# Attention, routed experts and a dense MLP on one Trainium2 core: the last MLP's matrix operands moved to other start addresses in SBUF

## The chip, the cores and the metric

One core of a Trainium2 chip runs the whole program. The metric is the device time of one execution in microseconds (us), less is better. The profile is one execution of the same program, recorded instruction by instruction.

## The reference

The program computes three stages, one after the other; the change touches the third.

```python
x = attention(q, k, v)                      # linear attention, 8 batches x 576 tokens, 512 wide
x = moe(x)                                  # 4608 tokens, each through one of 8 experts, 512 -> 1024 -> 512
h = x @ w_in                                # last MLP: 4608 x 512 by 512 x 2048
g = np.maximum(0.01 * h, h)
out = (g @ w_out).astype(np.float32)        # 4608 x 2048 by 2048 x 512
```

## The kernel before

Both products of the last MLP are split into a high and a low part (`hi`, `lo`, the type fp32r) and computed as hi*hi + hi*lo + lo*hi, so each block product is three matmuls per 128 rows of the contraction. On top of that each product is a Strassen-like scheme: 7 block products in the place of 8, numbered 1 to 7 and always run in the order 1, 2, 6, 7, 5, 3, 4 (`ORDER`).

A matmul has two operands in SBUF. `lhsT`, 128x128, is loaded into the array first (the profile shows this as an instruction of its own, PEld); `rhs`, here 128x256, is streamed through it. Every matmul of both products has its own load.

**The first product** (line L954, in `Hidden.product`) loads the weights and streams the tokens. It runs in units (m, q): 9 groups m of 512 tokens, and for each of them 4 quarters q of the weights. A unit is 7 products of 12 matmuls, 84 matmuls in all, and there are 36 units. The streamed operands of the products 1, 2 and 6 lie in the tile `x3`, those of 7, 5, 3 and 4 in `xh7`, `xl7`, `xh5` and so on. The loaded weights lie in `wi0` for q = 0 and in `wi1` for q = 1, 2, 3. The split into hi and lo is ScalarE's (L506) and VectorE's (L507).

**The second product** (line L1126, in `run` of `last_product`) loads the hidden values and streams the weights. It runs over 18 blocks s of 256 tokens; a block is 7 products of 24 matmuls, 168 in all. The two first blocks are interleaved, the others run one after the other. The loaded operand goes through a ring of three pairs of buffers (`ring`), made of spent parts of `wi0` and `x3`. The streamed weights lie in `wi0` (product 1), in `wi1` (products 2, 6, 7, 5) and in `wo3` and `wo4` (products 3 and 4). All these views are made in `views`.

**The token numbers**: the result rows are scattered by number. Per block a DMA loads 256 numbers into `idf[s % 2]` (L1078 in `load`), VectorE turns them into integers (`idi`, L1142), and GpSimd's indirect DMA scatters two times 128 rows (L1148).

The order of the work around the change is the order of the code; nothing is scheduled by costs. Tiles get their start addresses from pools: `pre` is laid out from the upper end of SBUF downwards (so its first tile is `xr0`, then `x3`, then `wi0` at the top), `pa`, `pa2` and `pb` one after the other from below.

The experts of the second stage (L663, L674) use the same type and the same three-matmul scheme with 512 streamed columns, in tiles named `xk`, `xv`, `xq`; their last, small groups run with 256 columns.

Of the kernel before, what the change touches and what calls it, by code (L numbers as in the profile page):

```python
# [9 lines left out]
F32 = mybir.dt.float32  # L10
# [22 lines left out]
C_ID, C_ONE, C_TRI, C_WD, C_EOFF, C_TOK, C_RST, C_K512, C_IOTA, C_E = 0, 128, 256, 384, 456, 464, 500, 740, 752, 768  # L33
# [856 lines left out]
class Hidden:  # L890
# [7 lines left out]
    def early(self, p, pw):  # L898
        self.xr[0] = p.tile([128, 4, 2 * TB], F32, name="xr0")
        self.x3 = p.tile([128, 3, 2, 2, TB], F32R, name="x3")  # L900
        for n, i in enumerate((1, 2, 6)):
            self.xh[i], self.xl[i] = self.x3[:, n, 0], self.x3[:, n, 1]
        self.w0 = pw.tile([128, 7, 1024], F32R, name="wi0")
        self.weights(self.w0, 0)

    def late(self, p, p2, ps):
        self.ps = ps
        self.w1 = p.tile([128, 21, 1024], F32R, name="wi1")
        for q in range(1, 4):
            self.weights(self.w1[:, 7 * q - 7:7 * q], q)  # L910
        self.xt = p.tile([128, 4096], F32, name="xt")
        self.xr[1] = self.xt[:, 0:2048].rearrange("p (k t) -> p k t", k=4)
        self.t = {i: self.xt[:, 2048 + 512 * n:2560 + 512 * n].rearrange("p (k t) -> p k t", k=2) for n, i in enumerate((4, 5, 6, 7))}
        for i in (7, 5, 3, 4):
            self.operand(p2, i)
        self.ht = [[p2.tile([128, 2, 2, TB], F32, name=f"ht{f}{i}") for i in range(3 - f)] for f in range(2)]
        self.s = [{n: p2.tile([128, 2, TB], F32, name=f"s{n}{i}") for n in (1, 6, 7, 5)} for i in range(2)]
# [108 lines left out]
        store(u, 1)  # L1026


def last_product(tc, did, hd, wops, out):

    nc, V = tc.nc, tc.nc.vector
    w, hr, S, ring, sv, yo, idf, idi = {}, [None, None], {}, [], [], [], [], []
# [3 lines left out]
    def wview(i, t):  # L1036
        w[i] = t.rearrange("p (h k f) -> p h k f", h=2, k=8)

    def views(hidden, p):

        w0, w1, x3, xr0 = hidden.w0, hidden.w1, hidden.x3, hidden.xr[0]
        half = lambda t: t.rearrange("p (k t) -> p k t", t=128)
        hr[0] = hidden.xt.rearrange("p (c t) -> p c t", t=TB)
        hr[1] = flat(w1, 1).bitcast(F32).rearrange("p (c t) -> p c t", t=TB)
        wview(1, flat(w0, 0))
        for n, i in ((0, 2), (2, 6), (3, 7), (4, 5)):
            wview(i, flat(w1, n))
        S[0] = p.tile([128, 8, 128], F32, name="S5")
        for n in range(2):
            S[1 + n] = xr0[:, 2 * n:2 * n + 2].rearrange("p a (b t) -> p (a b) t", t=128)  # L1050
        x3 = [x3[:, n].rearrange("p h k t -> p (h k t)") for n in range(3)]
        ring.append((half(w0[:, 4]), half(w0[:, 5])))
        ring.append((half(x3[0]), half(x3[1])))
        ring.append((half(w0[:, 6]), half(x3[2])))
        idf.extend(p.tile([128, 2, 2], F32, name=f"idf{i}") for i in range(2))

    def tiles(p):
        for i in range(2):
# [57 lines left out]
    def run(ps):  # L1116
        for i in (7, 5, 3, 4):
            wload(i)
        for n, (s, i) in enumerate(seq):
# [23 lines left out]
            else:  # L1143
# [3 lines left out]
                for t in range(2):  # L1147
# [3 lines left out]
                    tc.add_to_no_dep_group("out", ins.ins)  # L1151

    return views, tiles, late, ended, tail, run


@with_exitstack
def build(ctx: ExitStack, tc, a, out):
# [6 lines left out]
    did = dram.tile([NT + SLOT, 2], F32, name="did")  # L1164
    wops = {"win": [dram.tile([128, 7, 2, 2, 256], F32, name=f"wid{q}") for q in range(4)],
            "wout": dram.tile([7, 128, 2, 8, 256], F32, name="wod")}
    hd = dram.tile([NA, 4, 2, 128, 1024], F32, name="hd")
# [7 lines left out]
    with tc.manual_schedule():  # L1175
        cf = con.tile([128, CW], F32, name="cf")
# [40 lines left out]
        with actx:  # L1217
            tail, sp = attention(actx, pools, tc, cst, a, region, xd, first)
# [4 lines left out]
        with ExitStack() as sctx, ExitStack() as bctx:  # L1223

            def pre():
                p = sctx.enter_context(tc.tile_pool(name="pre", bufs=1, side="right", reuse_waits="tile"))
                hidden.early(p, p)
                hidden.xload(0)

                def loads():  # L1230
                    for i in ORDER:
                        hidden.wload(0, i)
                        yield

                return loads(), lambda: (hidden.prep(0, 1), hidden.prep(0, 2))

            with ectx, ExitStack() as rctx:
                rest(rctx, pre)
            views, tiles, late, ended, tail, run = last_product(tc, did, hd, wops, out)
            p = bctx.enter_context(tc.tile_pool(name="pa", bufs=1, reuse_waits="tile"))  # L1240
            with ExitStack() as hctx:
                ps = hctx.enter_context(tc.tile_pool(name="ps_w", bufs=2, space=PSUM, reuse_waits="tile"))
                hidden.late(p, hctx.enter_context(tc.tile_pool(name="pa2", bufs=1, reuse_waits="tile")), ps)
                views(hidden, p)
                for i in ORDER:
                    hidden.wload(1, i)
                hidden.xload(1)
                hidden.sums(0)
                for i in (6, 7, 5, 3, 4):
                    hidden.prep(0, i)  # L1250
                hidden.run(ended, tail)
            p = bctx.enter_context(tc.tile_pool(name="pb", bufs=1, reuse_waits="tile"))
            late(p)
            tiles(p)
            run(bctx.enter_context(tc.tile_pool(name="ps_b", bufs=2, space=PSUM, reuse_waits="tile")))
# [23 lines left out]
```

## Time and profile before

| what | value |
|---|---|
| median of 3 runs | 1349.68 us (1348.0 to 1351.29) |
| the profiled execution's own time | 1349.73 us |
| its span (first to last instruction) | 1348.0 us |
| first matmul of the first product | 617.56 us after the span's start |
| matmuls in the program's trace | 9185, of which 3024 in each of the two products |
| mean granted TensorE clock | 0.987 |

A row of the timeline gives the start of a run of like instructions, its length, the engine, line and tiles, and the count. The end of a matmul in the profile is modelled, and neighbours overlap; so the time that a matmul costs is read from starts: the difference between the starts of two rows, divided by the matmuls that lie between them. Names drop the buffer number: `hp<-xh,wi` is a matmul into `hp` whose operands are an `xh` tile and a `wi` tile.

### The profile page before, as it was taken

To read this page: it belongs to the slowest core of one execution; us is meant where nothing else is said; L and a number is where in the kernel's file an instruction comes from. 1 tells how busy PE (TensorE), PEld (TensorE's weight loads), DVE (VectorE), ACT (ScalarE), POOL (GpSimd) and SP (SyncE) were. 2 spreads that over 40 slices of the span, in tenths; PEclk is the share of its full clock that TensorE was granted. 3 is DMA by queue.
4 is the path that set the end of the run, shared out by engine and by line. 5 is a ranking of instruction groups with operands and counts; after the bars stand their busy time and mean duration, and the time that the engine had idled before them with its cause. 6 is when DMAs were issued, how large, how long until landed. Compare 5 with 4: busy or idle time off the path is not lost.

```text
span 1348.0 us, 23450 instructions
## 1 busy us (share of the span) xinstructions
PE 1296.3 (96%) x9185; PEld 1213.5 (90%) x9185; DVE 1039.9 (77%) x1380; ACT 583.0 (43%) x914; POOL 347.2 (26%) x283
## 2 busy tenths in 40 slices
PE   6999698999999999998999999999999999999998
PEld 6888677888888877888999999999989999999998
DVE  5789766787778878557888888888778778787775
ACT  4566435554555555463333233333233333433332
POOL 2227841011101110111434334344311121122121
PEclk9999898999999999999999999999989999999999
DMA  9876337879879887878832333432985344453430
GB/s 369 349 288 202 126 111 248 261 254 299 259 256 311 281 279 243 284 240 308 312 120 118 141 141 126 156 127 95 381 337 187 114 139 143 125 156 118 132 112 32
DMA packets 146442, 279.04 MB, mean 207 GB/s; under 512 B 18192, under 2 KB 69904, under 8 KB 145424
## 3 DMA queue, kind: packets, MB, share of 16 engines
q1 hardware_dynamic: 121536, 207.93, 46.2%
q10 hardware_dynamic: 17232, 48.48, 9.1%
q0 software_dynamic: 7552, 21.02, 4.5%
q8 instruction: 75, 1.23, 0.4%
q14 instruction: 47, 0.39, 0.1%
HBM read 181.07 MB, written 96.32 MB: 206 GB/s over the span
## 4 chain that ended last, share of the span: by engine, by line
PE 24%; issue 22%; POOL 5%; DMA 2%; DVE 0%; POOLq 0%; ACT 0%; SPq 0%; ACTq 0%
PE hp L954 24%; POOL out L1148 4%; DMA wi<-wid 1%; DMA hd<-ht 1%; POOL s L999 0%; DVE ht L968 0%; POOLq L1148 0%; POOL s L1000 0%; POOLq L1275 0%; ACT s L998 0%; DVE ht L1004 0%; DVE ht L1008 0%; SPq L924 0%; POOL ht L980 0%; ACTq L965 0%
## 5 line engine op out<-in xcount | busy, mean ns | idle before, releaser
L954 PE MATMUL hp<-xh,wi 128*128 128x256 f32 x1152 | 209.9, 280 | 0.9 <-DMA wi<-wid 0.9
L663 PE MATMUL hp<-xq,xk 128*128 128x512 f32 (+1 forms) x640 | 189.6, 380 | 3.6 <-DVE xr L262 2.5
L954 PEld LDWEIGHTS hp<-xh,wi 128*128 128x128 f32 x1152 | 178.7, 188 | 1.1 <-ACT xh L506 1.1
L954 PE MATMUL hp<-x,wi 128*128 128x256 f32 x1296 | 162.9, 284 | 3.6 <-ACTq L864 3.6
L954 PEld LDWEIGHTS hp<-x,wi 128*128 128x128 f32 x1296 | 159.4, 191 | 3.8 <-ACTq L864 3.8
L954 PE MATMUL hp<-xl,wi 128*128 128x256 f32 x576 | 161.4, 280 | 0.0
L1126 PE MATMUL yp<-wi,x 128*128 128x256 f32 x944 | 157.5, 282 | 0.9 <-DVE x L507 0.9
L629 POOL DMA_INDIRECT xg<-xd,idi x44 | 54.2, 1233 | 360.6 <-ACT xq L665 200.5
L674 PE MATMUL yp<-xq,xk 128*128 128x512 f32 (+1 forms) x400 | 142.4, 385 | 0.8 <-DVE xq L666 0.8
L663 PEld LDWEIGHTS hp<-xq,xk 128*128 128x128 f32 x640 | 118.0, 188 | 26.7 <-DVE xr L262 2.9
L1126 PE MATMUL yp<-wi,wi 128*128 128x256 f32 x960 | 139.8, 280 | 0.0
L1148 POOL DMA_INDIRECT out<-yo,idx x36 | 60.4, 1677 | 300.0 <-DVE idx L1142 279.5
L507 DVE TENSOR_TENSOR xv<-st,xk 128x1024 fp32r<-128x1024 f32 x81 | 99.6, 1231 | 48.8 <-ACT xk L506 48.3
L1126 PEld LDWEIGHTS yp<-wi,x 128*128 128x128 f32 x944 | 131.8, 190 | 1.4 <-DVE x L507 1.4
L1126 PEld LDWEIGHTS yp<-wi,wi 128*128 128x128 f32 x960 | 128.4, 189 | 0.0
L674 PE MATMUL yp<-xq,xv 128*128 128x512 f32 (+1 forms) x320 | 121.8, 381 | 0.0
L663 PE MATMUL hp<-xq,xv 128*128 128x512 f32 (+1 forms) x320 | 121.1, 378 | 0.0
L968 DVE SCALAR_TENSOR_TENSOR ht<-ht 128x1024 f32<-128x1024 f32 x72 | 113.2, 1582 | 1.9
L954 PEld LDWEIGHTS hp<-xl,wi 128*128 128x128 f32 x576 | 108.3, 188 | 0.0
L999 POOL TENSOR_TENSOR s<-s,s 128x512 f32<-128x512 f32 x36 | 49.4, 1372 | 189.0 <-DVE s L996 99.1
L506 ACT CAST xk<-st 128x1024 fp32r<-128x1024 f32 x84 | 87.6, 1045 | 15.8 <-ACT y L680 8.8
L674 PEld LDWEIGHTS yp<-xq,xk 128*128 128x128 f32 x400 | 75.2, 189 | 14.9 <-DVE xq L666 1.2
(214 smaller groups left out, 2512.0 us busy)
## 6 DMA issues: line engine op xcount, KB each, us to landing
st<-in_w SPq DMA_DIRECT2D x88, 512.0 KB
hd<-ht ACTq DMA_DIRECT2D x72, 512.0 KB
xt<-hd SPq DMA_DIRECT2D x18, 1024.0 KB
wi<-hd SPq DMA_DIRECT2D x18, 1024.0 KB
wi<-wid SPq DMA_DIRECT2D x28, 512.0 KB
v<-in_v SPq DMA_DIRECT2D x16, 650.0 KB
wi<-wod SPq DMA_DIRECT2D x5, 2048.0 KB
k<-in_k SPq DMA_DIRECT2D x16, 576.0 KB
```

The costliest lines, as they stand in the source:

```text
L506: nc.scalar.copy(out=hi, in_=src)
L507: (eng or nc.vector).tensor_tensor(out=lo, in0=src, in1=hi.bitcast(F32), op=ALU.subtract)
L629: nc.gpsimd.indirect_dma_start(out=xg[:, t], out_offset=None, in_=xd[0:n], in_offset=bass.IndirectOffsetOnAxis(ap=idis[s % 2][:, t:t + 1], ...
L663: nc.tensor.matmul(hp[:, rows], lhsT=w[:, k, 128 * f:128 * f + 128], rhs=x[:, k, rows], start=(n == 0), stop=(n == 11))
L674: nc.tensor.matmul(yp[:, rows], lhsT=w[:, f, 128 * d:128 * d + 128], rhs=h[:, rows], start=(n == 0), stop=(n == 23))
L954: self.nc.tensor.matmul(bank[:, g], lhsT=w[:, h, k, 128 * g:128 * g + 128], rhs=x[:, k], start=(n == 0), stop=(n == 5))
L968: V.scalar_tensor_tensor(out=c, in0=c, scalar=0.01, in1=c, op0=ALU.mult, op1=ALU.max)
L999: G.tensor_tensor(out=s[6], in0=s[6], in1=s[5], op=ALU.add)
L1126: nc.tensor.matmul(bank, lhsT=x[:, k], rhs=w[i][:, h, k], start=(c == 0), stop=(c == 23))
L1148: ins = nc.gpsimd.indirect_dma_start(out=out, out_offset=bass.IndirectOffsetOnAxis(ap=idi[s % 2][:, t:t + 1], axis=0), in_=y[:, t], in_off ...
```

## The change

Three edits: the pool `pre` gets a further tile of 96 bytes in a partition that nothing uses; the two tiles of token numbers `idf0` and `idf1` are no longer made, their place is the 8 first columns of a region of the constants (a triangle of ones, read once at the program's start into another tile); and that region is passed on.

```diff
@@ class Hidden, early
         self.w0 = pw.tile([128, 7, 1024], F32R, name="wi0")
         self.weights(self.w0, 0)
+        pw.tile([128, 24], F32, name="pad")
@@ last_product
-def last_product(tc, did, hd, wops, out):
+def last_product(tc, did, hd, wops, out, room):
...
-        idf.extend(p.tile([128, 2, 2], F32, name=f"idf{i}") for i in range(2))
+        idf.extend(room[:, 4 * i:4 * i + 4].rearrange("p (a b) -> p a b", a=2) for i in range(2))
@@ build
-            views, tiles, late, ended, tail, run = last_product(tc, did, hd, wops, out)
+            views, tiles, late, ended, tail, run = last_product(tc, did, hd, wops, out, cf[:, C_TRI:C_TRI + 128])
```

No instruction is added, removed or moved: the two built programs hold the same instructions in the same order on every engine, with the same waits. What differs is where tiles start. The table gives the start in a partition in bytes, and the remainder by 128; every slice that a matmul takes starts a multiple of 512 bytes further, so that the remainder is that of each operand.

| tile | use in matmuls | start before | by 128 | start now | by 128 |
|---|---|---|---|---|---|
| `x3` | first product, streamed (1, 2, 6); second, loaded (ring) | 188384 | 96 | 188288 | 0 |
| `wi0` | first product, loaded (q = 0); second, loaded (ring) and streamed (1) | 200672 | 96 | 200576 | 0 |
| `wi1` | first product, loaded (q = 1, 2, 3); second, streamed (2, 6, 7, 5) | 20352 | 0 | 20352 | 0 |
| `xh7` to `xl4`, 8 tiles | first product, streamed (7, 5, 3, 4) | 126912 and on | 64 | 126848 and on | 0 |
| `wo3`, `wo4` | second product, streamed (3, 4) | 126912, 143296 | 64 | 126848, 143232 | 0 |
| `xk`, `xv`, `xq` of the experts | loaded and streamed | 49664 to 146944 | 0 | the same | 0 |

`xr0`, which no matmul reads, goes from 96 to 0, and the tiles of `pa2` and `pb` for VectorE, ScalarE, GpSimd and DMAs (`ht`, `s`, `v`, `yo`, `idx`, `S7`) shift down by 64 bytes.

## Rows read from the trace of the kernel before

**Rows 1.** The page: busy time by engine, and the granted clock in 40 slices.
```profile
PE 1296.3 (96%) x9185; PEld 1213.5 (90%) x9185; DVE 1039.9 (77%) x1380; ACT 583.0 (43%) x914; POOL 347.2 (26%) x283
...
PEclk9999898999999999999999999999989999999999
```
**Rows 2.** Busy time by stretch, inside the first product and inside the second.
```profile
core 0: us, PE busy (x) PEld busy (x) DVE busy (x) ACT busy (x) POOL busy (x), PEclk, DMA share, GB/s
780.00:980.00 200.00, 200.00 (x1686) 200.00 (x1685) 163.50 (x190) 64.91 (x111) 82.35 (x61) 1.00 0.46 176
1010.00:1200.00 190.00, 190.00 (x1613) 190.00 (x1612) 150.95 (x185) 71.91 (x76) 34.47 (x20) 1.00 0.45 140
```
**Rows 3.** What TensorE waited for, 617 to 976 us and 975 to 1348 us.
```profile
PE hp L954 <- ACTq L864: 3.6, 1, 3.6
PE hp L954 <- DMA wi<-wid: 0.9, 1, 0.9
...
PE yp L1126 <- ACT wi L506: 2.2, 1, 2.2
PE yp L1126 <- DVE x L507: 0.9, 2, 0.5
```
**Rows 4.** Timeline of TensorE: two units of the first product, q = 3 and q = 0.
```profile
770.03 4.48 PE L954 MATMUL hp<-x,wi 128*128 128x256 f32 x36
774.35 0.28 PE L954 MATMUL hp<-xh,wi 128*128 128x256 f32 x1
...
780.01 4.48 PE L954 MATMUL hp<-x,wi 128*128 128x256 f32 x36
784.32 0.28 PE L954 MATMUL hp<-xh,wi 128*128 128x256 f32 x1
...
790.01 4.48 PE L954 MATMUL hp<-x,wi 128*128 128x256 f32 x36
```
**Rows 5.** Timeline of TensorE: one block of the second product, and the next one's start.
```profile
1105.10 3.03 PE L1126 MATMUL yp<-wi 128*128 128x256 f32 x24
1107.97 2.98 PE L1126 MATMUL yp<-wi,x 128*128 128x256 f32 x24
...
1113.60 2.98 PE L1126 MATMUL yp<-wi,wi 128*128 128x256 f32 x24
1116.42 2.98 PE L1126 MATMUL yp<-wi,x 128*128 128x256 f32 x24
1119.24 0.40 PE L1126 MATMUL yp<-wo,wi 128*128 128x256 f32 x2
...
1122.08 3.00 PE L1126 MATMUL yp<-wo,wi 128*128 128x256 f32 x24
1124.92 1.35 PE L1126 MATMUL yp<-wi,x 128*128 128x256 f32 x10
```
**Rows 6.** Timeline of TensorE: 256-column matmuls of the experts' last group.
```profile
589.48 0.40 PE L663 MATMUL hp<-xq,xk 128*128 128x256 f32 x2
589.72 0.28 PE L663 MATMUL hp<-xq,xv 128*128 128x256 f32 x1
...
599.56 0.40 PE L663 MATMUL hp<-xq,xk 128*128 128x256 f32 x2
599.80 0.28 PE L663 MATMUL hp<-xq,xv 128*128 128x256 f32 x1
```
**Rows 7.** Timeline of VectorE in the second product: a split of each ring buffer, the numbers' copy.
```profile
1108.45 1.23 DVE L507 TENSOR_TENSOR x<-xt,wi 128x1024 fp32r<-128x1024 f32 x1 [1.19 <-ACT wi L506]
1109.67 1.23 DVE L507 TENSOR_TENSOR wi<-xt,wi 128x1024 fp32r<-128x1024 f32 x1
...
1123.06 0.16 DVE L1142 CAST idx<-idf 128x2 int32<-128x2 f32 x1
```
**Rows 8.** Who waited for line L1142, the copy of the token numbers.
```profile
L1142 DVE CAST idx<-idf x18: 158/159/161, 1011.0 to 1340.6; 128x2 int32<-128x2 f32 x18
...
  POOL out L1148: 279.5, 18
```

## The prediction

> **What bounds the kernel now.** The page comes first [rows 1]: TensorE is busy 96% of the span, and the granted clock is near full nearly everywhere. Next come two stretches inside the last MLP [rows 2]: TensorE's busy time fills each to the last digit (200.00 of 200.00 us, 190.00 of 190.00), the clock is 1.00 (the 2.4 GHz level), and VectorE, the next busiest, has 163.50 and 150.95 us. Third, what TensorE waited for [rows 3]: 4.5 us in all in the first product, 3.1 us in the second, all at their beginnings. So from 617.56 us to the end the time is the sum of what 6048 matmuls cost, and a nanosecond (ns) on each of them is 6 us. Last, the pace, from differences of starts. The reader is to see that it is not the same everywhere, though type, shape and clock are.
>
> - First product, unit q = 3 [rows 4]: 36 matmuls that stream `x3` take 774.35 − 770.03 = 4.32 us, 120.0 ns each; the 48 that stream `xh`, `xl` take 780.01 − 774.35 = 5.66 us, 117.9 each. Unit q = 0, loaded from `wi0`: 4.31 us, 119.7 each, and 790.01 − 784.32 = 5.69 us, 118.5 each. A unit is 9.98 us (770.03 to 780.01) or 10.00 (780.01 to 790.01).
> - Second product, one block [rows 5]: product 1 takes 1107.97 − 1105.10 = 2.87 us, 119.6 ns each; products 2 and 6 together 1113.60 − 1107.97 = 5.63, 117.3; 7 and 5 together 1119.24 − 1113.60 = 5.64, 117.5; 3 and 4 together 1124.92 − 1119.24 = 5.68, 118.3. The block is 19.82 us.
> - Experts with 256 columns [rows 6]: from 589.48 to 599.56 us lie 28 groups of three, 84 matmuls in 10.08 us: 120.0 each.
>
> Against the starts of the two operands (remainders by 128, from the table of the change; loaded first, then streamed): (0, 96) 120.0; (0, 64) 117.9; (96, 96) 119.6 and 119.7; (96, 64) 118.3 and 118.5; (96, 0) 117.3 to 117.5; and (0, 0), the experts, 120.0.
>
> **The change part by part.** After it all 6048 matmuls are (0, 0). This pair occurs before only in the experts [rows 6], with the same type, width, clock level and three-matmul order. Two readings of the list are possible. One looks at the streamed start alone: 96 is slow, 64 better, 0 best; the experts don't fit. The other looks at both: where loaded and streamed operand have the same remainder the pace is 120, (96, 96) in the products and (0, 0) in the experts, and it is lower only in pairs that differ; (0, 96) is then a pair that gains nothing. I take the second: it leaves no row out, and its price is a row of just the state that the change makes.
>
> *First product.* A unit at 120.0 is 84 × 0.120 = 10.08 us. Of 36 units, 9 (q = 0) go from 10.00 to 10.08 and 27 from 9.98 to 10.08: 9 × 0.08 + 27 × 0.10 = 3.4 us more. Its streamed `x3` matmuls, which the change frees from 96, gain nothing by this reading; those of `xh`, `xl` lose.
>
> *Second product.* A block at 120.0 is 168 × 0.120 = 20.16 us against 19.82: 0.34 us, and 18 blocks give 6.1 us. The low end is product 1's own pace there, which is (96, 96) but only 119.6 [rows 5]: 168 × 0.1196 = 20.09, 18 × 0.27 = 4.9 us. I take 120.0, since product 1 follows a product of another pair and the experts' run is uniform, as the products will be.
>
> TensorE has no idle time that could take this in [rows 2]; the waits of [rows 3] stand at the beginnings and are set by other engines, so I leave them.
>
> TensorE's loads and streams meeting in SBUF is what this amounts to. The Trainium skill speaks against it: "TensorE: Matmul & The Clock Gate", section "Step-by-step: what each phase is for", has two independent read ports, and loading the next weights takes no read bandwidth from the running matmul; its gap for 256 columns at the high clock is 256 / 2.4 + 2.5 = 109 ns and knows no address. By that rule the sum would be 0; the trace disagrees at least in that there are paces from 117.3 to 120.0 at one width and clock [rows 4 to 6].
>
> *The token numbers.* Their DMA is the same, into another place, with the same waits; the copy is 0.16 us, 18 times, on VectorE [rows 7, 8], which is idle for about 39 us of the second stretch [rows 2]. Only the scatter waits for it, which TensorE does not wait for [rows 3]: nothing. If the numbers came late, only GpSimd's scatters would, except the last.
>
> *The other shifted tiles.* VectorE's split takes 1.23 us whether it writes `x3` or `wi0` and whatever it reads [rows 7]; nothing is taken for it. Should VectorE's work get some per cent slower, its 36 and 39 idle us [rows 2] cover it, and if faster nobody waits for it but at the second product's start (0.9 us [rows 3], the bound either way). The weight load that TensorE waited 0.9 us for [rows 3] lands in a tile that moves; that is its bound either way too.
>
> **Sum:** 3.4 + 6.1 = 9.5 us, on the profiled execution's 1349.73 us: **1359.2 us**, slower by 0.7%. That execution lies on the median of the runs (1349.68), so nothing is corrected. Own range of this case: from 3.4 + 4.9 less the two bounds of 0.9, which is 1356.2, to 9.5 plus 0.9 and the upper run's distance of 1.6, which is 1361.7.
>
> **The rivals.**
>
> *Faster: the streamed start alone sets the pace.* For it: within the two products the order 96, 64, 0 gives 120.0, 118.3 and 117.4 without exception, and (0, 96) = 120.0 needs no excuse. Against it: the experts, streamed at 0, run at 120.0 [rows 6]. It must hold that something else of theirs costs: by 512 bytes they start at 0, the changed operands at 384, as `wi1` does now. Price at 117.4 ns: a unit 9.86 us (84 × 0.1174) instead of 9.98 or 10.00, so 27 × 0.12 + 9 × 0.14 = 4.5 us; a block 19.72 instead of 19.82, so 18 × 0.10 = 1.8 us; together 6.3 us less: 1343.4 us. The point that decides: today's mean pace is (27 × 9.98 + 9 × 10.00 + 18 × 19.82) / 6048 = 118.4 ns; if (0, 0) at these addresses runs below that, the sign turns.
>
> *No difference.* Either the pace doesn't hang on the addresses at all but on which product follows which, or (0, 0) settles near 118.4, say with the first matmuls of a product quick and the rest at 120. 0.2% of the time, 2.7 us, is about what a measurement of this kernel tells from no change; it is 0.45 ns a matmul, so this case is a pace of 117.9 to 118.8: about 1349.7 us. The page's rule above gives this time too. Against it: the paces repeat with the operands' tiles, not with places in the order: product 1 with `wi0` is slow in both stretches, product 2 slow in the first product where it streams `x3`, quick in the second where it streams `wi1` [rows 4, 5]. That the change doesn't do what it says is excluded by the table of starts.
>
> **How the numbers follow.** Same remainders slow, as forecast: 0.69. Streamed start alone: 0.23; it has the plain order in its favour, and the experts' row against it is of other tiles. Nothing to see: 0.08. These are the chances of slower, faster and same. To leave out no more than 2 in 10 the range has to reach the faster case: from 1343.0 to 1361.7 us.
>
> **What would show it.** In the changed profile: the unit 10.08 us and the block 20.16 us, all products alike at 120.0 ns. The faster rival shows 9.86 and 19.72, alike at 117.4. Both products unlike each other would mean that more than the remainder by 128 counts. VectorE's and the DMAs' waits for the numbers should read as before; a new wait of TensorE of more than a us would make the working wrong whatever the pace.

## The result, and the profile after

| | before | after |
|---|---|---|
| median, runs on the same chip | 1348.0 us (1346.89 to 1351.29, 5 runs) | 1358.94 us (1357.59 to 1361.05, 5 runs) |
| ratio | | 1.0067, 95% interval 1.0052 to 1.0081 |
| span of the profiled execution | 1347.96 us | 1357.12 us |
| start of the first product, of the second, of the last matmul | 617.56, 979.61, 1342.75 us | 616.30, 983.20, 1351.91 us |

The change makes the kernel slower by 0.7%: 9.0 us of 1348.0 by the ratio, 10.9 by the two medians. All line numbers after L900 are one higher than before.

The page, and the two stretches of [rows 2]:

```profile
PE 1304.4 (96%) x9185; PEld 1221.4 (90%) x9185; DVE 1041.1 (77%) x1380; ACT 583.4 (43%) x914; POOL 348.3 (26%) x283
...
PEclk9999898999999999998999999999999999999999
```

```profile
780.00:980.00 200.00, 200.00 (x1669) 200.00 (x1668) 162.97 (x189) 64.29 (x111) 81.56 (x60) 1.00 0.44 169
1010.00:1200.00 190.00, 189.36 (x1579) 189.16 (x1578) 149.20 (x182) 71.58 (x76) 34.82 (x20) 1.00 0.42 135
```

TensorE fills the first stretch as before, at the same granted clock of 1.00, but with 1669 matmuls where [rows 2] has 1686. The page's 96% tells nothing of this: an engine whose every instruction got longer looks as busy as ever.

TensorE's timeline, the same two units of the first product as in [rows 4], then a block of the second product as in [rows 5]:

```profile
771.52 4.48 PE L955 MATMUL hp<-x,wi 128*128 128x256 f32 x36
775.84 0.28 PE L955 MATMUL hp<-xh,wi 128*128 128x256 f32 x1
...
781.60 4.48 PE L955 MATMUL hp<-x,wi 128*128 128x256 f32 x36
785.92 0.28 PE L955 MATMUL hp<-xh,wi 128*128 128x256 f32 x1
...
791.68 4.48 PE L955 MATMUL hp<-x,wi 128*128 128x256 f32 x36
```

```profile
1110.11 3.04 PE L1127 MATMUL yp<-wi 128*128 128x256 f32 x24
1112.99 3.04 PE L1127 MATMUL yp<-wi,x 128*128 128x256 f32 x24
...
1130.27 1.00 PE L1127 MATMUL yp<-wi,x 128*128 128x256 f32 x7
```

A unit is 10.08 us (771.52 to 781.60 to 791.68), a block 20.16 us (1110.11 to 1130.27). Inside them all is alike: 36 matmuls in 4.32 us, 48 in 5.76, 24 in 2.88 (1110.11 to 1112.99), each 120.0 ns.

What TensorE waited for, first product and then second, and who waited for the copy of the token numbers:

```profile
PE hp L955 <- ACTq L864: 3.5, 1, 3.5
PE hp L955 <- DMA wi<-wid: 0.8, 1, 0.8
PE hp L955 <- DVE ht L969: 0.2, 1, 0.2
```

```profile
PE yp L1127 <- ACT wi L506: 2.5, 2, 2.0
PE yp L1127 <- DVE x L507: 1.4, 2, 0.8
PE yp L1127 <- DVE wi L507: 0.8, 1, 0.8
```

```profile
L1143 DVE CAST idx<-cf x18: 157/158/160, 1014.3 to 1349.7; 128x2 int32<-128x2 f32 x18
...
  POOL out L1149: 284.5, 18
```

The waits are those of [rows 3] with 1.6 us more at the start of the second product (4.7 instead of 3.1 in all, the new one behind VectorE's `wi` 0.8); the numbers' copy is 158 ns and waited for as in [rows 8].

The 9.16 us between the spans are made of three differences of the starts above. The first product takes 366.90 us instead of 362.05 (+4.85), the second 368.71 instead of 363.14 (+5.57), and the first product begins 1.26 us earlier.

### The profile page after: what moved, and what is told of

Read it like the earlier page. It is cut to its first block, busy times and chain, and to the rows that moved or that the text cites. A ratio compares the mean times of both kernels' runs of the same rounds, so it can differ in the third digit from the quotient of the medians.

```text
span 1357.1 us, 23450 instructions
## 1 busy us (share of the span) xinstructions
PE 1304.4 (96%) x9185; PEld 1221.4 (90%) x9185; DVE 1041.1 (77%) x1380; ACT 583.4 (43%) x914; POOL 348.3 (26%) x283
## 3 DMA queue, kind: packets, MB, share of 16 engines
q8 instruction: 75, 1.23, 0.4%
## 4 chain that ended last, share of the span: by engine, by line
PE 24%; issue 23%; POOL 5%; DMA 2%; DVE 0%; POOLq 0%; ACT 0%; SPq 0%; ACTq 0%
PE hp L955 24%; POOL out L1149 4%; DMA wi<-wid 1%; DMA hd<-ht 1%; POOL s L1000 0%; DVE ht L969 0%; POOLq L1149 0%; POOL s L1001 0%; POOLq L1276 0%; ACT s L999 0%; DVE ht L1005 0%; DVE ht L1009 0%; SPq L925 0%; POOL ht L981 0%; ACTq L966 0%
## 5 line engine op out<-in xcount | busy, mean ns | idle before, releaser
L955 PE MATMUL hp<-xh,wi 128*128 128x256 f32 x1152 | 213.5, 283 | 0.8 <-DMA wi<-wid 0.8
L955 PEld LDWEIGHTS hp<-xh,wi 128*128 128x128 f32 x1152 | 182.4, 192 | 1.0 <-ACT xh L506 1.0
L1127 PE MATMUL yp<-wi,wi 128*128 128x256 f32 x960 | 142.8, 283 | 1.2 <-DVE wi L507 0.8
L663 PEld LDWEIGHTS hp<-xq,xk 128*128 128x128 f32 x640 | 117.8, 188 | 26.8 <-DVE xr L262 3.1
L1000 POOL TENSOR_TENSOR s<-s,s 128x512 f32<-128x512 f32 x36 | 49.4, 1373 | 193.4 <-ACT s L999 117.5
```

What stands on the lines that cost most here:

```text
L663: nc.tensor.matmul(hp[:, rows], lhsT=w[:, k, 128 * f:128 * f + 128], rhs=x[:, k, rows], start=(n == 0), stop=(n == 11))
L955: self.nc.tensor.matmul(bank[:, g], lhsT=w[:, h, k, 128 * g:128 * g + 128], rhs=x[:, k], start=(n == 0), stop=(n == 5))
L1000: G.tensor_tensor(out=s[6], in0=s[6], in1=s[5], op=ALU.add)
L1127: nc.tensor.matmul(bank, lhsT=x[:, k], rhs=w[i][:, h, k], start=(c == 0), stop=(c == 23))
```

## The experiments

Each timed kernel ran beside the kernel before on the same chip, and ratios are taken against that. That neighbour's median was between 1342.4 and 1348.6 us from one comparison to the next, so a time here is compared only with its own neighbour.

### Pairs of starts, by themselves

A program of matmuls alone: for each pair of starts 12 matmuls to begin with, then 48 with the pair, every one with its own load.

```python
for k, (n, s, m) in enumerate(pairs()):          # columns, loaded start, streamed start
    for count, nm in ((WARM, "warm"), (RUN, name(n, s, m))):
        t = ps.tile([128, n], F32, tag="b%d%d" % (k % 2, count == RUN), name=nm)
        for j in range(count):
            nc.tensor.matmul(t, lhsT=w[:, s + 128 * (j % 16):s + 128 * (j % 16) + 128],
                             rhs=x[:, m + n * (j % 8):m + n * (j % 8) + n], ...)
```

> Measured by itself, the pace of fp32r matmuls by the start of both operands. This kernel computes nothing of the reference: it fills two tiles with numbers of one input, runs 12 + 48 matmuls for each pair of starts (a load of 128 columns before each), and writes one tile of sums to all rows of the output. The loaded operand starts at 0, 16, 32, 64 or 96 bytes past a multiple of 128, the streamed one at steps of 4 or 16 bytes; 256 columns, and eight pairs with 512. Theory 1 (the two starts against each other): streamed = loaded gives 120.0 ns at 0, 32, 64 and 96 alike, also where they differ by whole multiples of 128 bytes; loaded 0 with streamed 64 gives 117.8, loaded 96 with streamed 0 gives 117.4, loaded 96 with streamed 64 gives 118.3, and what counts is the difference of the two by 128, so that all pairs with a difference of 32 give 117.4 and all of 64 give 117.8. Theory 2 (the streamed start alone): the pace is the same for all loaded starts. For 512 columns: 226.7 ns at (0, 0) as in the experts; by theory 1 some ns less where the starts differ, by theory 2 as well only if the start is other than 0.

TensorE's timeline; the letters behind y are loaded and streamed start in words of 4 bytes (a = 0, i = 32 bytes, C = 112), and a pace is the distance to the next "warm" row by 48:

```profile
218.18 5.60 PE L50 MATMUL yaC<-x,w 128*128 128x256 f32 x48
223.62 1.63 PE L50 MATMUL warm<-x,w 128*128 128x256 f32 x12
...
260.97 5.92 PE L50 MATMUL yii<-x,w 128*128 128x256 f32 x48
266.73 1.59 PE L50 MATMUL warm<-x,w 128*128 128x256 f32 x12
```

(32, 32) is 5.76 / 48 = 120.0 ns, (0, 112) is 5.44 / 48 = 113.3, and so is (64, 0). For starts at multiples of 32 bytes the pace follows the difference, streamed less loaded, by 256:

| difference | 0 | 32 | 64 | 96 | 128 | 160 | 192 | 224 |
|---|---|---|---|---|---|---|---|---|
| ns, 256 columns | 120.0 | 116.7 | 117.8 | 120.0 | 118.6 | 117.4 | 113.3 | 118.3 |

Equal starts give 120.0 at 32, 64 and 96 as at 0, so the slow thing is not the multiple of 128. (The row of (0, 0) is the first group of the program and begins with seven steps of 205 to 214 ns, at the 1.2 GHz level of the clock; from the fourteenth step on it too runs at 120.0.) The period is 256 bytes, not the 128 by which the prediction sorted the pairs: (0, 128) is 118.6, (0, 256) 120.0. By 256 the starts before were `x3` and `wi0` 224, `wi1` 128, `xh` and `wo` 192, and the table gives every pace of the kernel before to 0.4 ns:

| operands (loaded, streamed) | difference | by the table | measured in [rows 4, 5] |
|---|---|---|---|
| `wi1`, `x3` | 96 | 120.0 | 120.0 |
| `wi1`, `xh` | 64 | 117.8 | 117.9 |
| `wi0`, `x3`; ring, `wi0` | 0 | 120.0 | 119.7, 119.6 |
| `wi0`, `xh`; ring, `wo` | 224 | 118.3 | 118.5, 118.3 |
| ring, `wi1` | 160 | 117.4 | 117.3 to 117.5 |

The changed kernel has 0 everywhere, since all its tiles start at 128 by 256.

### The token numbers alone

```diff
-        idf.extend(p.tile([128, 2, 2], F32, name=f"idf{i}") for i in range(2))
+        idf.extend(room[:, 4 * i:4 * i + 4].rearrange("p (a b) -> p a b", a=2) for i in range(2))
```

Without the further tile, `xh` and `wo` move to 0 (by 128), `x3` and `wi0` stay at 96.

> The second edit alone: the numbers' tiles are moved, the 96 bytes at the top are not added. Starts by 128: xh to xl and wo3, wo4 at 0, x3 and wi0 stay at 96, wi1 at 0. Theory 1 (starts against each other): in units with q = 1 to 3 the 48 matmuls of xh, xl become (0, 0), 120.0 ns, x3 stays at (0, 96), 120.0: unit 10.08 us against 9.98; in q = 0 they become (96, 0), 117.4: 9.94 against 10.00; in the second product products 3 and 4 become (96, 0), 117.4: block 19.78 against 19.82. Sum 27 x 0.10 - 9 x 0.06 - 18 x 0.04 = +1.4 us. Theory 2 (streamed start alone): xh, xl at 117.4 in all units, 9.95 for q = 1 to 3; sum about -2 us.

1351.51 us (9 runs) against 1348.64 (18): ratio 1.0020, 1.0008 to 1.0033. The unit is 10.07 us for q = 1 to 3, 9.96 for q = 0, the block 19.775. That is the differences again: `xh` behind `wi1` goes from 64 to 0 and loses 2 ns, behind `wi0` and with `wo` behind the ring from 224 to 160 and gains 1. This part of the change makes the first product slow and would make the second a little quicker.

### The upper tiles alone

```diff
+        pw.tile([128, 24], F32, name="pad")
...
+        p2.tile([128, 16], F32, name="padc")
...
+        p.tile([128, 16], F32, name="padd")
```

`x3` and `wi0` go to 0 and tiles of 64 bytes keep `xh` and `wo` at 64. One tile `s1` and the numbers lie in the constants to make room.

> The first edit alone: x3 and wi0 at 0, wi1 at 0, xh to xl and wo3, wo4 at 64 as in the kernel before (to make room, one of the first product's s1 tiles and the token numbers lie in the spent constants, and 64 bytes are left free below). Theory 1 (starts against each other): first product: x3 (0, 0), 120.0, xh and xl (0, 64), 117.8, in all units: 9.97 us; second: products 1, 2, 6, 7, 5 (0, 0) at 120.0, products 3 and 4 (0, 64) at 117.8: block 20.06 against 19.82, 18 x 0.24 = +4.3 us, units -0.3 us, together about +4 us. Theory 2 (streamed start alone): x3 at 117.4, unit 9.88; block 19.75: together about -4.5 us.

1354.36 us (10 runs): ratio 1.0037, 1.0022 to 1.0053. The unit is 9.98 us, the block 20.06. Product 7 and the start of product 5 in one block:

```profile
1115.94 3.04 PE L1129 MATMUL yp<-wi,wi 128*128 128x256 f32 x24
1118.82 3.04 PE L1129 MATMUL yp<-wi,x 128*128 128x256 f32 x24
```

These 24 take 2.88 us, 120.0 ns each, where [rows 5] has 117.5. Here the second product is slow: `wi1` behind the ring goes from 160 to 0. Its streamed start never moved; only the loaded one did, which by the rival of the streamed start alone changes nothing. Each part of the change is a loss by itself.

### All starts equal at 64

```diff
-        pw.tile([128, 24], F32, name="pad")
+        pw.tile([128, 8], F32, name="pad")
...
+        p.tile([128, 16], F32, name="pad1")
```

(Against the changed kernel.) All matmul tiles at 64 by 128.

> As the changed kernel, but all operands start at 64 past a multiple of 128 (32 bytes less at the top, 64 bytes free ahead of wi1). Theory 1 (starts against each other): equal starts again, 120.0 ns everywhere, unit 10.08, block 20.16, the time of the changed kernel, about 9.5 us over the kernel before. Theory 2 (streamed start alone): streamed at 64, 117.9 to 118.3 everywhere: unit 9.92, block 19.85, about 2 us below the kernel before.

1359.63 us (4 runs): ratio 1.0066, 1.0040 to 1.0092, units 10.08 us, blocks 20.16, every matmul 120.0: the changed kernel's numbers at another remainder.

### More differences, and 512 columns

The first program with streamed starts from 128 to 252 bytes, other loaded starts, and 512 columns.

> As the first kernel of pairs (it too computes nothing of the reference), with other pairs: 256 columns, loaded at 0, streamed at 128 to 252 bytes by steps of 4; five pairs with other loaded starts; and 512 columns, loaded at 0, streamed at 0 to 248 by steps of 8, and six pairs more. Theory 1, as the first kernel of pairs left it: the pace is a function of streamed minus loaded start by 256 bytes. So with 256 columns 128 gives 118.6, 160 gives 117.4, 192 gives 113.3, 224 gives 118.3, and so do (128, 64) and (192, 128) give 113.3 and (192, 0) at a difference of 64 gives 117.8. Theory 2, the streamed start alone, would give (128, 64) and (0, 64) the same 117.8. With 512 columns equal starts give 226.7 at 0, 64 and 128 alike; whether a difference gives less than 226.7 is open: the eight pairs measured so far don't (228.8 to 234.2).

```profile
131.69 5.60 PE L49 MATMUL yaabq<-x,w 128*128 128x256 f32 x48
137.13 1.64 PE L49 MATMUL warm<-x,w 128*128 128x256 f32 x12
...
282.72 11.04 PE L49 MATMUL zaaaa<-x,w 128*128 128x512 f32 x48
293.60 2.96 PE L49 MATMUL warm<-x,w 128*128 128x512 f32 x12
```

(0, 192) is 113.3 ns, and so are (128, 64), with 112 (64, 176) and (96, 208), and (0, 144). (192, 128), which is 192 too, is 117.8: a first sign of what came later, passed over here. Nothing at 256 columns is below that, and the slowest is 123.3, at streamed starts that are multiples of 4 bytes only. With 512 columns it is the other way round: equal starts, here (0, 0), are the quickest at 10.88 / 48 = 226.7 ns, at 64 and at 128 as well, and all differences cost 2 to 13 ns more, up to 240.0 at 88 bytes.

### All matmuls at the difference 192

```diff
-        self.x3 = p.tile([128, 3, 2, 2, TB], F32R, name="x3")
+        self.x3f = p.tile([128, 12 * TB + 80], F32R, name="x3")
...
-            x3 = [x3[:, n].rearrange("p h k t -> p (h k t)") for n in range(3)]
+            x3 = [hidden.x3f[:, 32 + 1024 * n:32 + 1024 * n + 1024] for n in range(3)]
+            r0 = {n: hidden.w0f[:, 16 + 1024 * n:16 + 1024 * n + 1024] for n in (4, 5, 6)}
...
+        p2.tile([128, 48], F32, name="padc")
```

Padding puts `xh` and `x3` 192 behind the weights; in the second product the ring lies in the same tiles at starts shifted by 128 and 64 bytes, so that the loaded operands again differ from the streamed ones by 192.

> The kernel with all 6048 matmuls of the last MLP at a difference of 192 bytes (streamed minus loaded, by 256): x3 and xh to xl at 64, wi0, wi1, wo3 and wo4 at 128, the ring's views at 192, by shifting tiles and by views that begin 64 or 128 bytes later. Theory 1: 113.3 ns everywhere, unit 9.52 us against 9.98, block 19.04 against 19.82: 36 x 0.46 + 18 x 0.78 = 30.6 us below the kernel before, about 1318 us, if VectorE (8.2 us of work in a unit, 15.8 in a block) and the loads keep up; a few us more if they don't. Theory 2 (streamed start alone, by 128): the streamed operands are at 64 in the first product, 0 in the second: 117.9 and 117.4, about 1345 us.

1333.26 us (1323.65 to 1341.29, 12 runs): ratio 0.9926, 0.9899 to 0.9954. In the profile of its quickest execution units are 9.52 us and blocks 19.04 (84 and 168 at 113.3), but the two first blocks take 57.00 us where they took 46.24. And the time of that execution, 1323.65 us, is one of six between 1323.7 and 1328.7; the six others lie between 1337.8 and 1341.3, which one pace for one difference does not explain. TensorE's waits at the start of the second product, and ScalarE's timeline there:

```profile
PE yp L1131 <- ACT wi L506: 12.5, 2, 10.1
```

```profile
977.56 0.37 ACT L1135 COPY v<-yp 128x256 f32<-128x256 f32 x1 [14.31 <-DMA hd<-ht]
977.83 1.05 ACT L506 CAST wi<-xt 128x1024 fp32r<-128x1024 f32 x1
```

ScalarE's copy into `v10` waited 14.31 us for the DMA out of a tile `ht`, and the splits that TensorE needed stood behind it. The padding had moved `v10` onto the last 192 bytes of the old `ht11`. This is the sort of wait that the prediction feared of moved tiles; the changed kernel's profile has none like it.

### 192 without the overlap

```diff
+        p.tile([128, 48], F32, name="pade")
```

> The kernel with a difference of 192 bytes, with 192 bytes left free ahead of the second product's v tiles, so that v no longer lies over the end of the tile whose store is the last of the first product. Theory (the wait of 10.1 us at the second product's start came from that overlap: ScalarE's copy into v waited for the store hd<-ht): the wait goes, the first two blocks take 45 to 47 us instead of 57.0, units stay 9.52 and blocks 19.04, and the time is about 10 us under the run with the overlap, 27 to 31 us (2.0 to 2.3%) under the kernel before. Rival (the wait is the price of the faster first product: the weights' loads or the stores come too late by their bandwidth): the first two blocks stay at 55 us or more.

1327.47 us (1317.91 to 1329.32, 5 runs) against 1343.51: ratio 0.9878, 0.9857 to 0.9898. The long wait goes, so the rival that the faster first product causes it falls. In the quickest execution units are 9.52 and blocks 19.04 as worked out, and the first two blocks take 49.06 us where 45 to 47 were expected. The median is 16.0 us under its neighbour, not the 27 to 31 expected. But the five times lie 11 us apart, and those of the kernel with the overlap 18, where the changed kernel and its parts have 3 to 7.

### The same program, two more executions

> The same kernel as the run before, for a second profile, since its five times lie between 1317.9 and 1329.3 us and the first profile is of the shortest. Theory: the pace is fixed by the starts (units 9.52, blocks 19.04 again), and what varies is the waits at the two places where TensorE waits for transfers, the first four units (42.7 us in the first profile) and the two first blocks (49.06 us). Rival: the pace itself differs between executions, and units or blocks in the middle are longer than 9.52 and 19.04.

> A third profile of the same kernel, with the same expectations: units 9.52 and blocks 19.04 in the middle, and differences only at the two beginnings.

1325.25 and 1334.58 us beside 1342.38. Rows of the timeline, of the first of the two and then of the second: two unit starts, and two neighbouring products of a block.

```profile
750.77 4.40 PE L958 MATMUL hp<-x,wi 128*128 128x256 f32 x36
760.66 4.40 PE L958 MATMUL hp<-x,wi 128*128 128x256 f32 x36
...
1114.39 2.88 PE L1132 MATMUL yp<-wi,wi 128*128 128x256 f32 x24
1117.11 2.88 PE L1132 MATMUL yp<-wi,x 128*128 128x256 f32 x24
```

```profile
741.49 4.24 PE L958 MATMUL hp<-x,wi 128*128 128x256 f32 x36
751.01 4.24 PE L958 MATMUL hp<-x,wi 128*128 128x256 f32 x36
...
1115.71 2.99 PE L1132 MATMUL yp<-wi,wi 128*128 128x256 f32 x24
1118.54 2.99 PE L1132 MATMUL yp<-wi,x 128*128 128x256 f32 x24
```

One has units of 9.89 us (117.8 ns) and blocks at 2.72 / 24 = 113.3; the other units of 9.52 and blocks at 117.8 (19.79 us each), to the last block. So my theory of one pace for one difference falls: at 192 there are two, and a product of the MLP keeps the one that it settles on near its beginning. A whole product at the slower pace costs some 13 us (36 × 0.37, or 18 × 0.75), which is the distance between the two groups of times of the kernel with the overlap (means of 1325.8 and 1338.7). That this is their cause is not shown, since none of its slower executions was profiled.

### One product of each unit and block at the difference 0

```diff
-        self.x3 = self.x3f[:, 0:12 * TB].rearrange("p (n h k t) -> p n h k t", n=3, h=2, k=2)
+        self.x3 = [self.x3f[:, o:o + 1024].rearrange("p (h k t) -> p h k t", h=2, k=2) for o in (16, 1088, 2112)]
...
-        wview(1, flat(w0, 0))
+        wview(1, hidden.w0f[:, 16:16 + 4096])
```

> As the run e7, but in every unit and every block product 1 has equal starts (difference 0, the pace that has been 120.0 in every profile), the other six a difference of 192. Theory 3 (at 192 there are two lasting paces, 113.3 and 117.8, and which one holds is decided when the stream of matmuls starts after a wait): each unit and block enters the 192 anew, out of the same pace of 120, so all units are alike, and so are all blocks, in every execution; if the entry falls on the quick pace, unit 12 x 0.120 + 72 x 0.1133 = 9.60 us, block 24 x 0.120 + 144 x 0.1133 = 19.20, and the time about 1316 us with a spread under 5 us in the runs; if it falls on the other, 9.92 and 19.84, about 1345. Rival (the pace is drawn by the execution, not by the entry): units of 9.60 in one stretch and 9.92 in another, and times as far apart as in e7 (11 us).

1322.81 us (1321.78 to 1325.33, 5 runs) against 1343.65: ratio 0.9852, 0.9838 to 0.9866. The spread is 3.5 us instead of 11. In the profile all units but the first and the fourth are 9.60 us, and all blocks but the two first 19.20:

```profile
749.74 4.32 PE L958 MATMUL hp<-x,wi 128*128 128x256 f32 x36
759.34 4.32 PE L958 MATMUL hp<-x,wi 128*128 128x256 f32 x36
...
1142.09 3.02 PE L1132 MATMUL yp<-wi 128*128 128x256 f32 x24
1144.95 2.90 PE L1132 MATMUL yp<-wi,x 128*128 128x256 f32 x24
...
1150.41 2.88 PE L1132 MATMUL yp<-wi,wi 128*128 128x256 f32 x24
1153.13 2.88 PE L1132 MATMUL yp<-wi,x 128*128 128x256 f32 x24
```

Product 1 runs at 2.86 / 24 = 119.2 ns, the others come back to 113.3 behind it each time (1150.41 to 1153.13). The slow product costs 0.08 us a unit and 0.16 a block, and the case of 117.8 (about 1345 us) came in none of the five runs. The 1316 us expected did not come either: units and blocks alone would give 36 × 0.38 + 18 × 0.62 = 24.8 us less than before, measured are 20.8, since the fourth unit (12.58 us, before 11.15) and the two first blocks (46.75, before 46.24) gained nothing.

### Each difference after waits

The first program without the 12 matmuls ahead; instead each group of 41 waits some us for VectorE, ten times with growing waits.

> Pairs again, without the reference's computation: ten differences (0 to 224 by 32, 112 and 144), each ten times with 41 matmuls, and ahead of each time TensorE has to wait for VectorE, by waits of ten lengths. Theory 3: a difference of 0 gives 120.0 ten times of ten; 192 gives 113.3 in some and 117.8 in others; which of the others have two paces is open. Rival: one pace per difference, as the first two kernels of pairs showed, where nothing waited.

TensorE's timeline at 192; the bracket is the wait ahead of the group:

```profile
523.62 4.93 PE L53 MATMUL yy<-x,w 128*128 128x256 f32 x41 [2.16 <-DVE x L50]
530.93 5.09 PE L53 MATMUL yy<-x,w 128*128 128x256 f32 x41 [2.38 <-DVE x L50]
```

4.93 us is a first step of 0.22, then steps that come down to 113.3 ns, and the last one's 0.28; in 5.09 the steps come to 117.8. So with the same operands a start after a wait can lead to either pace. The two groups differ in the wait, in the copies on VectorE that make it and in the output buffer, and three other groups with the second one's buffer have 113.3; what it is in the wait that decides stays open. Groups of 6.5 us and more ran for a part at the 1.2 GHz level (213 ns a matmul) and are left out. Of the groups at the full clock, by the last 24 steps, difference 0 has 120.0 in every one, 64 has 117.8, 96 has 120.0, 192 has 113.3 six times and 117.8 once, 32 has 116.7 or 117.8, 144 has 116.7 or 118.7, and 112 has 113.3 in all six.

### All matmuls at the difference 112

```diff
-        self.x3 = self.x3f[:, 0:12 * TB].rearrange("p (n h k t) -> p n h k t", n=3, h=2, k=2)
+        self.x3 = self.x3f[:, 4:12 * TB + 4].rearrange("p (n h k t) -> p n h k t", n=3, h=2, k=2)
...
-        p2.tile([128, 48], F32, name="padc")
+        p2.tile([128, 208], F32, name="padc")
+        self.xf = p2.tile([128, 4096 + 8], F32R, name="xh")
```

(Against the kernel at 192.) All of `x3` and `xh`, and the views of the second product's weights, start 16 bytes into their tiles.

> All 6048 matmuls at a difference of 112 bytes (streamed less loaded start, remainder by 256), by padding tiles and by views that start 16 bytes into their tile; the work is otherwise that of the changed kernel. The matmuls alone, after waits, gave 113.3 ns at 112 in every clean repetition, where 192 gave 113.3 or 117.8. Theory (the difference alone sets the pace, and 112 has one pace where 192 has two): units 84 x 0.1133 = 9.52 us, blocks 19.04 us in every stretch, 36 x (9.98 - 9.52) + 18 x (19.82 - 19.04) = 30.6 us less than before, some 3 back for the start of the second product: 1315 to 1320 us, and runs within 4 us of each other. Rival one (112 has two paces like 192): runs spread over 10 us and more, median 1325 to 1335. Rival two (16-byte starts cost something of their own in the kernel, with fp32r tiles that VectorE and ScalarE write): units above 9.6 us throughout, or VectorE's splits above 1.23 us and new waits of TensorE.

1329.17 us (1327.51 to 1330.85, 4 runs) against 1348.03: ratio 0.9855, 0.9829 to 0.9880. Rows of two usual units, a late one, and two neighbouring products of a block:

```profile
768.62 4.24 PE L960 MATMUL hp<-x,wi 128*128 128x256 f32 x36
...
778.14 4.24 PE L960 MATMUL hp<-x,wi 128*128 128x256 f32 x36
...
902.42 4.40 PE L960 MATMUL hp<-x,wi 128*128 128x256 f32 x36
...
912.10 4.24 PE L960 MATMUL hp<-x,wi 128*128 128x256 f32 x36
...
1144.47 2.88 PE L1137 MATMUL yp<-wi,wi 128*128 128x256 f32 x24
1147.19 2.88 PE L1137 MATMUL yp<-wo,x 128*128 128x256 f32 x24
```

The paces are as expected, units 9.52 us, every block from the third on 19.04 (113.3), and the runs within 3.3 us. So neither rival shows: there is no second pace, and VectorE's splits still take 1.23 us. The time was not: 18.9 us less than its neighbour where 27 were expected. I had counted the gain on all 36 units and 18 blocks. Two of the first units take 12.58 and 13.22 us, more than the 11.58 and 11.15 of before (the granted clock is 0.51 from 620 to 625 us, in the first); the last third of the units has six of 9.66 to 9.77 (902.42 to 912.10 is one), in three neighbouring pairs, where the second unit's first weight load waits 0.17 to 0.29 us for VectorE's L998, which reads an `hp` tile, and some ten matmuls behind the wait are slower; and the first two blocks take 49.73 us instead of 46.24. TensorE at 113.3 ns waits there for what did not get faster: the second product's splits 6.9 us in all, and the weights of the first units 1.5.

This kernel and the one with product 1 at 0 are the quickest by their medians, alike in their ratios, and beat both kernels of the case: 0.985 of before, and by 0.9852 / 1.0067 some 0.979 of the changed one.

## Why the prediction was right

*The mechanism: equal starts are slow.* Right. Units of 10.08 and blocks of 20.16 us, alike at 120.0 ns, are what the prediction said would show it, and the kernels with one part of the change and with all starts at 64 give what equal starts should, each.

*The pair (0, 96) "gains nothing".* Right, but left without a reason, and the reason shows that the order by 128 was one half of the truth: by 256 it is the difference 96, which runs at 120.0 with other starts too, at (16, 112). Equality by 128, as the prediction had it, would have got (0, 128) wrong, 118.6 ns; neither kernel of the case has such a pair.

*The first product's 3.4 us.* It was 4.85. The pace gave its part; 1.3 us of the rest are two units at the beginning: the first took 12.65 us instead of 11.58, the fourth 11.53 instead of 11.15, against the 0.1 each that the sum had. The first unit's part is a lower granted clock, 0.52 instead of 0.90 between 615 and 620 us. It is not the change's: with the token numbers alone the same unit took 12.73 us, with the upper tiles alone 11.55, and in three executions of one program, the kernel at 192 without the overlap, 9.64, 11.29 and 11.27.

*The second product's 6.1 us.* It was 5.57. The pace was sized right, 16 blocks by 0.345 are 5.5 us, but the two first blocks, interleaved, did not grow by their share of 0.7: 46.27 us against 46.24. They are not alike inside. The stretch from 990 to 995 us, before and then after, with two rows of before:

```profile
990.00:995.00 5.00, 5.00 (x27) 5.00 (x27) 3.81 (x4) 2.99 (x4) 0.00 (x0) 0.55 1.00 425
990.00:995.00 5.00, 3.08 (x23) 2.88 (x24) 3.50 (x3) 1.65 (x3) 0.00 (x0) 1.00 1.02 433
```

```profile
989.28 0.63 PE L1126 MATMUL yp<-wi 128*128 128x256 f32 x2
...
989.92 0.63 PE L1126 MATMUL yp<-wi 128*128 128x256 f32 x2
```

Before, TensorE came out of its wait into a granted clock of 0.55, most of it at the 1.2 GHz level, and some 24 matmuls cost 213 ns each (three in 0.64 us), 2.3 us more than at the usual pace. After, the clock is 1.00 there, but TensorE waits 1.6 us more. These are the terms that the sum did not have: the pace of the steady state was laid over stretches that the waits and the clock behind them set.

*The sum, 9.5 us.* 9.16 between the profiles, 9.0 by the ratio: 1.45 too little for the first product and 0.5 too much for the second, and the first product happened to begin 1.26 us earlier, which no part of the change explains. So the agreement to 0.4 us is partly luck; that the units and the blocks came out to the digit is not.

*The token numbers, the shifted tiles: nothing.* Right here [rows 7, 8]: the copy takes 158 ns as before, and no new wait of TensorE reaches the microsecond that the prediction named as a sign of being wrong. That such a shift can cost 10 us was seen when padding laid `v10` over the end of an `ht` tile.

*The rival of the streamed start alone* fell with the upper tiles alone, where the block went up to 20.06 us though of its streamed starts only product 1's had moved. *The rival of no difference* wanted a pace of 117.9 to 118.8 ns after the change, or one that follows the order of the products; the order is the same, and all products now run at 120.0. The Trainium skill ("TensorE: Matmul & The Clock Gate", "Step-by-step: what each phase is for"), which the prediction put beside this rival, has two independent read ports, so that a load takes no bandwidth from the stream, and a formula that gives 109 ns for 256 columns, an estimate, with no term for an address. The runs show something else: 113.3 to 123.3 ns at one width and clock, by the addresses of the two operands, and with the upper tiles alone a loaded start that moved cost the other operand's stream 2.5 ns a matmul. What makes the difference count, no run here shows.

## What to carry to other kernels

Where TensorE is the bound and each matmul has its own load, read the pace of single tiles from starts in the timeline, and compare it between tile pairs of one shape: a busy share of 100% here hid 6%. Aligned tiles are not a goal in themselves: with 256 streamed columns equal starts are among the slow cases here (120.0 ns against 113.3 at a difference of 112 or 192 bytes), with 512 they are the quickest, so the pairs are measured, at the width in use, and in more than one execution. And a tile moved by some bytes can come to lie on the end of an old one: look for a new wait on the owner of that place.

## What the runs showed of the hardware

- The pace of fp32r matmuls, each with its own load, hangs on the difference of the operands' starts by 256 bytes: with 256 columns at the 2.4 GHz level 113.3 to 120.0 ns for starts at multiples of 32 bytes, and up to 123.3 between.
- A difference can have two lasting paces (192: 113.3 and 117.8 ns), kept for over 300 us; the groups after waits show that a start after a wait can lead to either. Times of one program then differ by 11 us or more with no wait that would explain it, and with one product in seven at equal starts the spread of five runs was 3.5 us. At a difference of 112 no second pace was seen.
